# A new order for the first ten slots of a fused top-k attention and gated feed-forward kernel

## The chip, the cores and the metric

The kernel runs on one core of a Trainium2 chip. The core has five engines that work side by side, each through its own queue of instructions: TensorE (PE in the profile) multiplies matrices and loads weights for it (PEld), VectorE (DVE) and GpSimd (POOL) work on elements, ScalarE (ACT) evaluates functions and copies, SyncE (SP) starts transfers. The metric is the time of one execution on the device in microseconds (us), lower is better; a time given for a kernel is the median of its runs.

## The reference

There are 8 batches of 8 heads, 576 positions and 64 elements a head. For each query row the 576 scores are cut to the 32 largest, a softmax runs over those, and the values are summed with it. The heads of one position then stand side by side as a row of 512, and a feed-forward layer follows: 512 to 2048, a gate h * sigmoid(1.702 h), 2048 to 512.

```python
scores = scale * np.matmul(q, k.transpose(0, 1, 3, 2))          # (8, 8, 576, 576)
kth = np.partition(scores, -top_k, axis=-1)[..., -top_k:-top_k + 1]   # top_k = 32
scores = np.where(scores >= kth, scores, -1000000000.0)
attn = np.exp(scores - np.max(scores, axis=-1, keepdims=True))
attn = attn / (np.sum(attn, axis=-1, keepdims=True) + 1e-09)
x = np.matmul(attn, v)  # then (B, H, S, D) -> (B*S, H*D) = (4608, 512)
h = x @ w_in                                                    # (512, 2048)
g = h * (1.0 / (1.0 + np.exp(-1.702 * h)))
out = g @ w_out                                                 # (2048, 512)
```

## The kernel before

The work is cut into 144 slots, 18 for each batch. A slot is one tile of 128 query rows of a pair of heads (or the tails of two pairs). Five things are done with each slot's rows, in different slots of the program:

- **scores(n)**: 8 matmuls on TensorE and two copies out of PSUM on ScalarE.
- **topk(n)**: 14 operations on VectorE, eight MAX8 (each finds the 8 largest of 576) and six MATCH_REPLACE8 (each takes those out).
- **exponentials(n)** in slot n+1: two Prelu and two Exp on ScalarE, after the small bounds on GpSimd; then divide(n), which takes the reciprocal on VectorE in the middle of slot n+1's topk.
- **turn(n)** in slot n+1: the probabilities are transposed on TensorE and copied by ScalarE. In early slots the transposing matrix is the identity scaled by the reciprocals (`by`, made by GpSimd); in later ones it is the plain identity, and the probabilities are scaled before by ScalarE and GpSimd.
- **values(n)** in slot n+1: 10 matmul pairs on TensorE, one copy (xT) on ScalarE.

When the tiles of a row block are done, **hidden** computes a quarter of the feed-forward's first product per slot (16 matmuls), **tanh** and **gate** the gate in the slot after, and **project** a quarter of the second product (4 matmuls of 128x512) later. `to_project` is the queue in between. **prepare** transposes a pair of heads of q or k as it is loaded.

Both weight matrices, 32 pieces of 128x512, are loaded in the first slots and converted there into a form that TensorE takes: `size` (ScalarE), `shift` (VectorE), `sign` and `low` (ScalarE), and `finish` (two operations on GpSimd). A piece is loaded in the slot before its conversion, and finished in the slot after it. `by_slot` says how many pieces each slot converts.

Every engine works its queue in the order in which this program calls it, so the order of calls inside `slot(n)` is what the change is about. Blank lines are left out below, and cuts are marked.

```python
    SETTLED = 11
    # ... cut ...
    raws = pool("raws", 8)
    loads = pool("loads", 2)
    vals = pool("vals", 6)
    qkt = pool("qkt", 6)
    scp = pool("scp", 3)
    prp = pool("prp", 2)
    lefts = pool("lefts", 1)
    small = pool("small", 4)
    ptp = pool("ptp", 2)
    dgp = pool("dgp", 1)
    xtp = pool("xtp", 2)
    xtt = pool("xtt", 1)
    gtp = pool("gtp", 3)
    thp = pool("thp", 2)
    osp = pool("osp", 1)
    ps_s = pool("ps_s", 2, space=PSUM)
    ps_t = pool("ps_t", 2, space=PSUM)
    ps_h = pool("ps_h", 1, space=PSUM)
    ps_p = pool("ps_p", 1, space=PSUM)
    # ... cut ...
    pieces = [(c, g) for g in range(2) for c in range(CC)]
    for g in range(NG):
        pieces += [(c, g + 2) for c in range(CC) if g + 2 < NG] + [(None, f) for f in range(g * G, g * G + G)]
    # ... cut ...
    def round_piece(n):
        c, g = pieces[n]
        dst = wout[:, g, :] if c is None else win[:, c, g * PIECE : (g + 1) * PIECE]
        words = raw.pop(n)[:].rearrange("p (n w) -> p n w", w=2)
        low, high = words[:, :, 0], words[:, :, 1].bitcast(F32)
        bits, whole = dst.bitcast(U32), dst.bitcast(I32)
        def finish():
            nc.gpsimd.tensor_tensor(out=whole, in0=whole, in1=low.bitcast(I32), op=ALU.add)
            nc.gpsimd.tensor_tensor(out=dst, in0=dst, in1=high, op=ALU.mult)
        return {
            "size": lambda: nc.scalar.activation(dst, high, AF.Abs, scale=REBASE),
            "shift": lambda: nc.vector.tensor_scalar(bits, bits, 3, None, op0=ALU.logical_shift_left),
            "sign": lambda: nc.scalar.activation(high, high, AF.Sign),
            "low": lambda: nc.scalar.mul(out=low.bitcast(I32), in_=low, mul=2.0**-29),
            "finish": finish,
        }
    # ... cut ...
    def prepare(name, b, hp):
        src = loaded.pop((name, b, hp))
        before = 0 if name == "q" else TAIL
        dst = qkt.tile([P, S + before], F32, name=f"{name}_t")
        full = ps_t.tile([P, 512], F32, name="tp")
        for t in range(NF):
            nc.tensor.transpose(full[:, t * P : (t + 1) * P], src[:, t, :, :], ident[:])
        scale = SCALE if name == "q" else 1.0
        nc.scalar.mul(out=dst[:, before : before + FULL], in_=full[:], mul=scale)
        (qT if name == "q" else kT)[b, hp] = dst
        if name == "k":
            ends = ps_t.tile([P, 512], F32, name="tp")
            nc.tensor.transpose(ends[:, 0:P], loaded.pop(("ends", b, hp))[:], ident[:])
            nc.scalar.mul(out=qT[b, hp][:, FULL:S], in_=ends[:, 0:TAIL], mul=SCALE)
            for to in (0, before + FULL):
                nc.scalar.copy(out=dst[:, to : to + TAIL], in_=ends[:, TAIL:P])
    # ... cut ...
        sc = st[n]["sc"] = scp.tile([P, 2, S], F32, name="sc")
        for i in range(2):
            nc.scalar.copy(out=sc[:, i, :].rearrange("p (c k) -> p c k", c=2), in_=ps[i][:, :, 0:HALF])
    # ... cut ...
    def bounds(n):
        top = st[n]["top"]
        cut = st[n]["cut"] = small.tile([P, 2], F32, name="cut")
        low = st[n]["low"] = small.tile([P, 2], F32, name="low")
        nc.gpsimd.tensor_scalar(cut[:], top[:, :, TOPK - 1], -1.0, None, op0=ALU.mult)
        nc.gpsimd.tensor_tensor(out=low[:], in0=top[:, :, TOPK - 1], in1=top[:, :, 0], op=ALU.subtract)
    def exponentials(n):
        sc, cut, low = st[n]["sc"], st[n]["cut"], st[n]["low"]
        pr = st[n]["pr"] = prp.tile([P, 2 * S], F32, name="pr")
        den = st[n]["den"] = small.tile([P, 2], F32, name="den")
        for i in range(2):
            nc.scalar.activation(sc[:, i, :], sc[:, i, :], AF.Prelu, bias=cut[:, i : i + 1], alpha=HUGE)
        for i in range(2):
            nc.scalar.activation(
                pr[:, i * S : (i + 1) * S], sc[:, i, :], AF.Exp, bias=low[:, i : i + 1],
                accum_out=den[:, i : i + 1],
            )
    # ... cut ...
    def divide(n):
        den, pr = st[n]["den"], st[n]["pr"]
        some = small.tile([P, 2], F32, name="some")
        nc.vector.tensor_scalar_add(some[:], den[:], 1e-9)
        rden = small.tile([P, 2], F32, name="rden")
        nc.vector.reciprocal(rden[:], some[:])
        if n < SETTLED:
            by = st[n]["by"] = dgp.tile([P, 2, P], F32, name="by")
            for i in range(2):
                nc.gpsimd.tensor_scalar(by[:, i, :], ident[:], rden[:, i : i + 1], None, op0=ALU.mult)
        else:
            nc.scalar.activation(pr[:, 0:S], pr[:, 0:S], AF.Copy, scale=rden[:, 0:1])
            nc.gpsimd.tensor_scalar(pr[:, S : 2 * S], pr[:, S : 2 * S], rden[:, 1:2], None, op0=ALU.mult)
    # ... cut ...
    def tanh(aside):
        if to_gate:
            ph, g, rows = to_gate.pop()
            th = thp.tile([P, G, P], F32, name="th")
            nc.scalar.activation(th[:], ph[:], AF.Tanh, scale=0.851 / RAISE)
            if aside:
                h = raws.tile([P, G, P], F32, name="h", tag="raw")
                nc.scalar.copy(out=h[:], in_=ph[:])
                ph = h
            gated.append((th, ph, g, rows))
    def gate(aside):
        if not gated:
            return
        th, h, g, rows = gated.pop()
        gT = gtp.tile([P, G, P], F32, name="gT")
        if aside:
            nc.gpsimd.tensor_scalar(th[:], th[:], 1.0, None, op0=ALU.add)
            nc.gpsimd.tensor_tensor(out=gT[:], in0=th[:], in1=h[:], op=ALU.mult)
        else:
            nc.vector.scalar_tensor_tensor(
                out=gT[:], in0=th[:], scalar=1.0, in1=h[:], op0=ALU.add, op1=ALU.mult
            )
        to_project.append((gT, g, rows))
    # ... cut ...
    def project(blocks):
        if blocks[0] == 0:
            proj["on"] = to_project.pop(0)
    # ... cut ...
            ob = osp.tile([P, C], F32, name="ob")
            nc.scalar.mul(out=ob[:], in_=po[:], mul=0.5 / RAISE**2)
            for on, row in rows:
                nc.sync.dma_start(out[row : row + on.stop - on.start, :], ob[on, :])
    # ... cut ...
    by_slot = dict(enumerate([3, 4, 3, 4, 3, 4, 3, 4, 4]))
    # ... cut ...
            at(max(hp - 2, -1), load, name, 0, hp)
            at(max(hp - 2, -1), prepare, name, 0, hp)
    for hp in range(NP):
        at(hp - 1, load_v, 0, hp)
    for n in by_slot:
        for x in by_slot[n]:
            at(n - 1, load_piece, x)
    # ... cut ...
    def slot(n):
        todo = later.pop(n, [])
        for fn, args in todo:
            if fn is not prepare:
                fn(*args)
        preparing = [args for fn, args in todo if fn is prepare]
        settled = n > SETTLED
        aside = settled and n < N
        before = 0 <= n - 1 < N
        if before:
            bounds(n - 1)
            exponentials(n - 1)
        some = [round_piece(x) for x in by_slot.get(n, [])]
        for piece in some:
            piece["size"]()
        shifts = [piece["shift"] for piece in some]
        tanh(aside)
        for i, op in enumerate(topk(n) if 0 <= n < N else [lambda: None] * 14):
            op()
            if i == 2 and unfinished:
                unfinished.pop(0)()
            if i == 5:
                if before:
                    divide(n - 1)
                while unfinished:
                    unfinished.pop(0)()
            if i == 11 and not aside:
                gate(aside)
            if i > 6 and shifts:
                shifts.pop(0)()
        if aside:
            gate(aside)
        for args in preparing:
            prepare(*args)
        going = len(to_project) > (1 if n < N else 0)
        if going and settled:
            project(range(G - 1))
        if before:
            turn_main(n - 1)
        if going and settled:
            project(range(G - 1, G))
        if before:
            turn_ends(n - 1)
        for piece in some:
            piece["sign"]()
        if before:
            values(n - 1)
        for m in (0, 1) if n < 0 else (n + 2,):
            if m < N:
                scores(m)
        hidden()
        if going and not settled:
            project(range(G))
        for piece in some:
            piece["low"]()
            unfinished.append(piece["finish"])
    with tc.manual_schedule():
        for n in range(-1, N + 1):
            slot(n)
        n = N + 1
        while ready or to_gate or gated or to_project:
            slot(n)
            n += 1
```

Of the kernel before, what the change touches and what calls it, by code (L numbers as in the profile page):

```python
# [28 lines left out]
def kernel(  # L29
# [34 lines left out]
    CC = C // P  # L64
    FC = DFF // P
    G = 4
    NG = FC // G
# [4 lines left out]
    MAIN = (0, FULL + 2 * TAIL)  # L72
    SCALE = 1.0 / float(D) ** 0.5

    SETTLED = 11
    assert D == 64 and 2 * TAIL == P and C == NP * P and C == PIECE and B % 2 == 0
    assert TOPK == 32 and NP == 4 and NF == 4 and NG == 4 and CC == 4

# [1 line left out]
    pool = lambda name, bufs, **kw: ctx.enter_context(tc.tile_pool(name=name, bufs=bufs, **kw))  # L80
# [9 lines left out]
    dgp = pool("dgp", 1)  # L90
    xtp = pool("xtp", 2)
    xtt = pool("xtt", 1)
    gtp = pool("gtp", 3)
    thp = pool("thp", 2)
    osp = pool("osp", 1)
    ps_s = pool("ps_s", 2, space=PSUM)
# [7 lines left out]
    wout = const.tile([P, FC, C], F32, name="wout")  # L104


    pieces = [(c, g) for g in range(2) for c in range(CC)]
    for g in range(NG):
        pieces += [(c, g + 2) for c in range(CC) if g + 2 < NG] + [(None, f) for f in range(g * G, g * G + G)]
    raw = {}  # L110

    def load_piece(n):
# [8 lines left out]
# [26 lines that stand above are left out]
# [37 lines left out]
# [18 lines that stand above are left out]
# [8 lines left out]
    N = len(slots)  # L210
# [51 lines left out]
# [14 lines that stand above are left out]
# [5 lines left out]
# [3 lines that stand above are left out]
# [6 lines left out]
    def turn(n, first, cols, blocks):  # L290
# [5 lines left out]
        for c in range(blocks):  # L296
            at = slice(cols + c * P, cols + (c + 1) * P)
            if n >= SETTLED:
                nc.tensor.transpose(tp[:, c * P : (c + 1) * P], pr[:, at], ident[:])  # L299
# [15 lines left out]
    def turn_ends(n):  # L315

        turn(n, 2 * NF, FULL, 1)
# [3 lines left out]
    def values(n):  # L321
        b, t, hps = slots[n]
        pt = st[n]["pt"]
        outs = []
        for p in range(2 if t == NF else 1):
            cols = slice(p * TAIL, (p + 1) * TAIL) if t == NF else slice(0, P)
            main, tail = vv[b, hps[p]]
            o = ps_t.tile([P, 512], F32, name="o", tag="tp")
            for c in range(NF + 1):
                for j in range(2):  # L330
                    nc.tensor.matmul(  # L331
                        o[j * D : (j + 1) * D, 0 : cols.stop - cols.start],
                        lhsT=main[:, c, j, :] if c < NF else tail[:, j, :],
                        rhs=pt[:, j * NF + c if c < NF else 2 * NF, cols],
                        start=(c == 0),
                        stop=(c == NF),
                    )
            outs.append((o, hps[p]))
        for o, hp in outs:
            if t < NF:  # L340
                if (b, t) not in xts:
                    xts[b, t] = xtp.tile([P, CC, P], F32, name="xT")
                nc.scalar.copy(out=xts[b, t][:, hp, :], in_=o[:, 0:P])
            else:
                if (b // 2, t) not in xts:
                    xts[b // 2, t] = xtt.tile([P, CC, P], F32, name="xT_t")
                at = b % 2 * TAIL
                nc.scalar.copy(out=xts[b // 2, t][:, hp, at : at + TAIL], in_=o[:, 0:TAIL])
        if hps[-1] == NP - 1:
            if t < NF:  # L350
                ready.append((xts.pop((b, t)), [(slice(0, P), b * S + t * P)]))
            elif b % 2:
                rows = [(slice(i * TAIL, (i + 1) * TAIL), (b - 1 + i) * S + FULL) for i in range(2)]
                ready.append((xts.pop((b // 2, t)), rows))
        st[n].clear()
# [4 lines left out]
    to_gate, gated, to_project = [], [], []  # L360
# [77 lines left out]
    READY = (((-9, -8), (-7, -6), (-5, -4), (-3, -2)), ((-7, -6), (-5, -4), (-3, -3), (-2, -2)))  # L438
    FETCH = (((-13, -12), (-11, -10), (-7, -6), (-5, -4)), ((-11, -10), (-9, -8), (-6, -5), (-4, -3)))
    VALUES = ((-8, -7, -1, 0), (-8, -7, 0, 0))  # L440
    by_slot = dict(enumerate([3, 4, 3, 4, 3, 4, 3, 4, 4]))
    for n in by_slot:
        first = sum(map(len, list(by_slot.values())[:n]))
        by_slot[n] = list(range(first, first + by_slot[n]))
# [16 lines left out]
    unfinished = []  # L461
# [4 lines that stand above are left out]
            if fn is not prepare:  # L466
                fn(*args)
        preparing = [args for fn, args in todo if fn is prepare]
        settled = n > SETTLED
        aside = settled and n < N  # L470
        before = 0 <= n - 1 < N
        if before:
            bounds(n - 1)
            exponentials(n - 1)
        some = [round_piece(x) for x in by_slot.get(n, [])]
        for piece in some:
            piece["size"]()
# [14 lines that stand above are left out]
                shifts.pop(0)()  # L492
        if aside:
            gate(aside)
        for args in preparing:
            prepare(*args)
        going = len(to_project) > (1 if n < N else 0)
        if going and settled:
            project(range(G - 1))
        if before:  # L500
            turn_main(n - 1)
        if going and settled:
            project(range(G - 1, G))
        if before:
            turn_ends(n - 1)
        for piece in some:
            piece["sign"]()
        if before:
            values(n - 1)
        for m in (0, 1) if n < 0 else (n + 2,):  # L510
            if m < N:
                scores(m)
        hidden()
        if going and not settled:
            project(range(G))
        for piece in some:
            piece["low"]()
            unfinished.append(piece["finish"])

    with tc.manual_schedule():  # L520
        for n in range(-1, N + 1):
            slot(n)
        n = N + 1
# [33 lines left out]
```

## Time and profile before

| what | value |
|---|---|
| time, median of 3 runs | 1678.19 us (1676.68 to 1678.51) |
| span of the profiled run | 1674.9 us |
| VectorE busy in the profile | 1472.0 us |
| ScalarE busy | 1153.3 us |
| GpSimd busy | 746.3 us |
| one MAX8 or MATCH_REPLACE8 | 747 and 742 ns, next one starts some 70 ns before its end |
| matmuls of hidden, of project | 491.0 us in 4096 and 540.0 us in 1152 records |

In a line of the groups the profile names the line of the kernel, the engine, the operation, what it writes and what it reads, how often it ran, its busy time and the mean of one. A float32 product appears as two records, so 16 matmuls of `hidden` are 32 records. In a timeline the brackets hold the idle time before an instruction and who ended it. In a chain of waits each line is a start, a duration and what set the end in that stretch. TensorE's granted clock is given in tenths of full speed, or as a share of it.

### The profile page before, as it was taken

To read this page: it belongs to the slowest core of one execution; us is meant where nothing else is said; L and a number is where in the kernel's file an instruction comes from. 1 tells how busy PE (TensorE), PEld (TensorE's weight loads), DVE (VectorE), ACT (ScalarE), POOL (GpSimd) and SP (SyncE) were. 2 spreads that over 40 slices of the span, in tenths; PEclk is the share of its full clock that TensorE was granted. 3 is DMA by queue.
4 is the path that set the end of the run, shared out by engine and by line. 5 is a ranking of instruction groups with operands and counts; after the bars stand their busy time and mean duration, and the time that the engine had idled before them with its cause. 6 is when DMAs were issued, how large, how long until landed. Compare 5 with 4: busy or idle time off the path is not lost.

```text
span 1674.9 us, 32016 instructions
## 1 busy us (share of the span) xinstructions
PE 1599.7 (96%) x11945; PEld 1175.7 (70%) x11945; DVE 1472.0 (88%) x3212; ACT 1153.3 (69%) x2446; POOL 746.3 (45%) x783
## 2 busy tenths in 40 slices
PE   5577999999999999999999999999999999999999
PEld 3465767777777766777777776777777776777776
DVE  6898789998999997999899998999899998899990
ACT  6786566677766667667777776777776677666661
POOL 2776234444444443444444444444444443444440
PEclk7699999999999999999999999999999999999999
DMA  8342000111001110111001110011100110000000
GB/s 223 113 139 55 23 21 22 28 35 29 22 7 29 35 29 22 29 29 36 15 14 29 29 29 14 16 28 36 29 21 8 28 43 22 22 8 7 7 8 13
DMA packets 125723, 56.59 MB, mean 34 GB/s; under 512 B 116864, under 2 KB 116864, under 8 KB 125568
## 3 DMA queue, kind: packets, MB, share of 16 engines
q1 hardware_dynamic: 125568, 54.55, 12.3%
q8 instruction: 94, 1.54, 0.4%
q14 instruction: 61, 0.50, 0.1%
HBM read 45.09 MB, written 9.44 MB: 33 GB/s over the span
## 4 chain that ended last, share of the span: by engine, by line
PE 89%; ACT 6%; DVE 3%; issue 1%; SPq 1%; DMA 0%; POOL 0%; POOLq 0%
PE ph L372 29%; PE po L420 29%; PE o L331 10%; PE s_ps L224 10%; PE tp L299 8%; PE tp L301 2%; ACT pr L270 2%; PE tp L192 1%; ACT sc L231 1%; DVE top L240 1%; DVE left L243 1%; ACT sc L268 1%; ACT raw L144 1%; DVE wout L142 0%; ACT pr L287 0%
## 5 line engine op out<-in xcount | busy, mean ns | idle before, releaser
L240 DVE MAX8 top<-left 128x8 f32<-128x576 f32 x864 | 610.2, 747 | 0.0
L420 PE MATMUL po<-wout,gT 128*128 128x512 f32 x1152 | 540.0, 593 | 0.0
L288 POOL TENSOR_SCALAR pr<-pr,rden 128x576 f32<-128x576 f32 x133 | 229.5, 1725 | 683.3 <-ACT th L389 627.3
L372 PEld LDWEIGHTS ph<-xT,win 128*128 128x128 f32 x4096 | 467.2, 192 | 55.7 <-issue 47.4
L372 PE MATMUL ph<-xT,win 128*128 128x128 f32 x4096 | 491.0, 278 | 5.7 <-DVE gT L405 5.7
L243 DVE MATCH_REPLACE8 left<-top,left 128x576 f32<-128x576 f32 x576 | 423.3, 742 | 0.0
L309 ACT COPY pt<-tp 128x512 f32<-128x512 f32 (+1 forms) x432 | 193.5, 481 | 207.1 <-PE tp L299 183.0
L420 PEld LDWEIGHTS po<-wout,gT 128*128 128x128 f32 x1152 | 198.0, 191 | 143.5 <-issue 143.5
L231 ACT COPY sc<-s_ps 128x576 f32<-128x576 f32 x288 | 169.9, 642 | 130.1 <-PE s_ps L224 130.0
L270 ACT ACTIVATE pr<-sc,low 128x576 f32<-128x576 f32 x288 | 219.6, 768 | 0.0
L299 PEld LDWEIGHTS tp<-ident,pr 128*128 128x128 f32 x1197 | 142.9, 140 | 102.8 <-issue 41.5
L240 DVE MAX8 top<-sc 128x8 f32<-128x576 f32 x288 | 202.0, 743 | 13.8 <-ACT sc L231 13.8
L243 DVE MATCH_REPLACE8 left<-top,sc 128x576 f32<-128x576 f32 x288 | 211.6, 742 | 0.0
L268 ACT ACTIVATE sc<-sc,cut 128x576 f32<-128x576 f32 x288 | 208.7, 779 | 2.0 <-POOL cut L259 2.0
L402 POOL TENSOR_SCALAR th<-th 128x512 f32<-128x512 f32 x132 | 197.6, 1497 | 0.0
L224 PE MATMUL s_ps<-k_t,q_t 64*128 64x288 f32 (+1 forms) x1280 | 180.9, 430 | 1.2 <-ACT sc L231 0.7
L331 PEld LDWEIGHTS o<-pt,v_l 128*64 128x64 f32 x2560 | 127.9, 138 | 70.4 <-ACT pt L309 70.4
L299 PE MATMUL tp<-ident,pr 128*128 128x128 f32 x1197 | 174.6, 273 | 0.2 <-POOL pr L288 0.2
L403 POOL TENSOR_TENSOR gT<-th,h 128x512 f32<-128x512 f32 x132 | 168.9, 1280 | 11.0
L331 PE MATMUL o<-pt,v_l 128*64 128x128 f32 (+1 forms) x2560 | 161.8, 269 | 2.3 <-ACT pt L309 2.2
L279 DVE TENSOR_SCALAR some<-den 128x2 f32<-128x2 f32 x144 | 24.3, 169 | 147.4 <-ACT pr L270 147.3
L224 PEld LDWEIGHTS s_ps<-k_t,q_t 64*128 64x128 f32 (+1 forms) x1280 | 98.1, 177 | 41.0 <-issue 21.7
(50 smaller groups left out, 1171.3 us busy)
## 6 DMA issues: line engine op xcount, KB each, us to landing
q_l<-in_q_dram SPq DMA_DIRECT2D x64, 128.0 KB, 2.6
k_l<-in_k_dram SPq DMA_DIRECT2D x64, 128.0 KB, 2.6
v_l<-in_v_dram SPq DMA_DIRECT2D x64, 128.0 KB, 2.6
raw<-in_moe_w_in_dram SPq DMA_DIRECT2D x16, 512.0 KB, 4.7
raw<-in_moe_w_out_dram SPq DMA_DIRECT2D x16, 512.0 KB, 3.7
out_dram<-ob SPq DMA_DIRECT2D x32, 256.0 KB, 2.1
ends<-in_q_dram SPq DMA_DIRECT2D x32, 32.0 KB, 2.4
ends<-in_k_dram SPq DMA_DIRECT2D x32, 32.0 KB, 2.5
```

The lines of the kernel that those rows point to most:

```text
L224: nc.tensor.matmul(ps[i][rows, c, 0:HALF], lhsT=qT[b, hps[p]][on, cols], rhs=kT[b, hps[p]][on, FIRST[i] + c * HALF : FIRST[i] + (c + 1) * ...
L240: nc.vector.max(top[:, i, 8 * r : 8 * r + 8], (left if r else sc)[:, i, :])
L243: nc.vector.match_replace(left[:, i, :], top[:, i, 8 * r : 8 * r + 8], (left if r else sc)[:, i, :], LOWEST)
L268: nc.scalar.activation(sc[:, i, :], sc[:, i, :], AF.Prelu, bias=cut[:, i : i + 1], alpha=HUGE)
L270: nc.scalar.activation(pr[:, i * S : (i + 1) * S], sc[:, i, :], AF.Exp, bias=low[:, i : i + 1], accum_out=den[:, i : i + 1],)
L288: nc.gpsimd.tensor_scalar(pr[:, S : 2 * S], pr[:, S : 2 * S], rden[:, 1:2], None, op0=ALU.mult)
L299: nc.tensor.transpose(tp[:, c * P : (c + 1) * P], pr[:, at], ident[:])
L309: nc.scalar.copy(out=to, in_=tp[:, 0 : blocks * P])
L331: nc.tensor.matmul(o[j * D : (j + 1) * D, 0 : cols.stop - cols.start], lhsT=main[:, c, j, :] if c < NF else tail[:, j, :], rhs=pt[:, j * N ...
L372: nc.tensor.matmul(ph[:, i, :], lhsT=win[:, c, f * P : (f + 1) * P], rhs=xT[:, c, :], start=(c == 0), stop=(c == CC - 1),)
L402: nc.gpsimd.tensor_scalar(th[:], th[:], 1.0, None, op0=ALU.add)
L420: nc.tensor.matmul(po[:], lhsT=gT[:, i, :], rhs=wout[:, f, :], start=(f == 0), stop=(f == FC - 1))
```

## The change

The change reorders slots -1 to 9. It has four parts.

- **Scores first.** In slots -1 to 6 the preparation of a pair and the scores of slot n+2 come right after the exponentials, ahead of everything else. Before, they came after the values. In slot -1 each pair's scores follow its preparation directly.
- **Weight steps in ScalarE's waits.** `low` moves from the end of the slot to places ahead of `turn_main` (two pieces) and after `turn_ends` (the rest), where ScalarE would wait for TensorE. `sign` comes after the values' copy. The pieces are loaded in another order (three quarters of the first matrix, then a quarter of the second, and so on), and the slots take 2, 3, 4, 4, 4, 4, 3, 4, 4 pieces in place of 3, 4, 3, 4, 3, 4, 3, 4, 4.
- **Projections from slot 7 on, first in TensorE's slot.** Before, they began in slot 6 and stood last in TensorE's slot up to slot 11. Now they stand where the later slots have them, around `turn_main`. The queue `to_project` keeps two entries waiting and not one, so gT has four buffers and not three.
- **An earlier end of the early form.** Slots 9 and 10 of the probabilities are scaled ahead of a plain transpose, as all later ones; `SETTLED` goes from 11 to 9. The gate moves to GpSimd from slot 10 on, and not from slot 12 on.

The whole diff:

```diff
--- before.py
+++ after.py
@@ -72,7 +72,9 @@
     MAIN = (0, FULL + 2 * TAIL)
     SCALE = 1.0 / float(D) ** 0.5
 
-    SETTLED = 11
+
+    PROJECTS = 6
+    SETTLED = 9
     assert D == 64 and 2 * TAIL == P and C == NP * P and C == PIECE and B % 2 == 0
     assert TOPK == 32 and NP == 4 and NF == 4 and NG == 4 and CC == 4
 
@@ -90,7 +92,7 @@
     dgp = pool("dgp", 1)
     xtp = pool("xtp", 2)
     xtt = pool("xtt", 1)
-    gtp = pool("gtp", 3)
+    gtp = pool("gtp", 4)
     thp = pool("thp", 2)
     osp = pool("osp", 1)
     ps_s = pool("ps_s", 2, space=PSUM)
@@ -104,9 +106,8 @@
     wout = const.tile([P, FC, C], F32, name="wout")
 
 
-    pieces = [(c, g) for g in range(2) for c in range(CC)]
-    for g in range(NG):
-        pieces += [(c, g + 2) for c in range(CC) if g + 2 < NG] + [(None, f) for f in range(g * G, g * G + G)]
+    pieces = [(c, g) for g in range(NG - 1) for c in range(CC)] + [(None, f) for f in range(G)]
+    pieces += [(c, NG - 1) for c in range(CC)] + [(None, f) for f in range(G, FC)]
     raw = {}
 
     def load_piece(n):
@@ -438,7 +439,7 @@
     READY = (((-9, -8), (-7, -6), (-5, -4), (-3, -2)), ((-7, -6), (-5, -4), (-3, -3), (-2, -2)))
     FETCH = (((-13, -12), (-11, -10), (-7, -6), (-5, -4)), ((-11, -10), (-9, -8), (-6, -5), (-4, -3)))
     VALUES = ((-8, -7, -1, 0), (-8, -7, 0, 0))
-    by_slot = dict(enumerate([3, 4, 3, 4, 3, 4, 3, 4, 4]))
+    by_slot = dict(enumerate([2, 3, 4, 4, 4, 4, 3, 4, 4]))
     for n in by_slot:
         first = sum(map(len, list(by_slot.values())[:n]))
         by_slot[n] = list(range(first, first + by_slot[n]))
@@ -466,12 +467,22 @@
             if fn is not prepare:
                 fn(*args)
         preparing = [args for fn, args in todo if fn is prepare]
-        settled = n > SETTLED
-        aside = settled and n < N
+        settled = n > PROJECTS
+        aside = SETTLED < n < N
         before = 0 <= n - 1 < N
         if before:
             bounds(n - 1)
             exponentials(n - 1)
+        if n < 0:
+            for m in range(2):
+                for args in preparing:
+                    if args[2] == m:
+                        prepare(*args)
+                scores(m)
+        elif not settled:
+            for args in preparing:
+                prepare(*args)
+            scores(n + 2)
         some = [round_piece(x) for x in by_slot.get(n, [])]
         for piece in some:
             piece["size"]()
@@ -492,30 +503,30 @@
                 shifts.pop(0)()
         if aside:
             gate(aside)
-        for args in preparing:
-            prepare(*args)
-        going = len(to_project) > (1 if n < N else 0)
-        if going and settled:
+        if settled:
+            for args in preparing:
+                prepare(*args)
+        for piece in some[:2]:
+            piece["low"]()
+        going = settled and len(to_project) > (2 if n < N else 0)
+        if going:
             project(range(G - 1))
         if before:
             turn_main(n - 1)
-        if going and settled:
+        if going:
             project(range(G - 1, G))
         if before:
             turn_ends(n - 1)
+        for piece in some[2:]:
+            piece["low"]()
+        if before:
+            values(n - 1)
         for piece in some:
             piece["sign"]()
-        if before:
-            values(n - 1)
-        for m in (0, 1) if n < 0 else (n + 2,):
-            if m < N:
-                scores(m)
+            unfinished.append(piece["finish"])
+        if settled and n + 2 < N:
+            scores(n + 2)
         hidden()
-        if going and not settled:
-            project(range(G))
-        for piece in some:
-            piece["low"]()
-            unfinished.append(piece["finish"])
 
     with tc.manual_schedule():
         for n in range(-1, N + 1):
```

## The prediction

> **What bounds the kernel now.** I read the page's busy shares and its 40 slices first, then windows of equal length, then the chain of waits inside the first 170 us, then the timeline around the first slots.
>
> From the page of the kernel before (busy time by engine; then the span in 40 slices of 42 us, busy tenths, and the granted TensorE clock):
>
> ```profile
> PE 1599.7 (96%) x11945; PEld 1175.7 (70%) x11945; DVE 1472.0 (88%) x3212; ACT 1153.3 (69%) x2446; POOL 746.3 (45%) x783
> ...
> PE   5577999999999999999999999999999999999999
> PEclk7699999999999999999999999999999999999999
> ```
>
> TensorE is the bound from the fifth slice on. Only the first four slices, some 170 us, have holes, and the change lies in them. The windows (length, busy time of each engine, clock, DMA share, GB/s) say the same:
>
> ```profile
> 40.00:60.00 20.00, 8.03 (x52) 6.37 (x48) 16.80 (x33) 16.07 (x32) 14.76 (x16) 0.68 0.36 120
> 100.00:120.00 20.00, 16.72 (x118) 13.54 (x117) 19.83 (x42) 17.39 (x35) 16.48 (x19) 0.91 0.40 134
> 300.00:600.00 300.00, 300.00 (x2194) 220.56 (x2191) 277.47 (x613) 212.67 (x451) 134.29 (x140) 1.00 0.11 27
> ```
>
> At 40 to 60 us no engine is full: a ring of waits. At 100 to 120 VectorE is full (19.83 of 20). From 300 TensorE is. So the end is the moment at which TensorE becomes saturated, plus the TensorE work still undone then. The ring is in the chain (start, duration, what), slots 2 to 3:
>
> ```profile
> 52.27 2.13 PE o L331 x20
> 54.41 1.22 PE s_ps L224 x8
> 55.63 1.16 ACT sc L231 x2
> 56.79 1.67 ACT raw L144 x3
> 58.46 0.70 ACT sc L268 x2
> 59.16 0.52 issue
> 59.68 1.62 ACT pr L270 x4
> 61.33 0.18 DVE some L279
> ...
> 61.87 0.62 POOL by L285
> 62.48 0.04 issue
> 62.53 3.80 PE tp L301 x16
> ```
>
> Scores and their copies (1.22 + 1.16) stand in the ring between the values of one slot and the exponentials of the next. I call the start of a slot's first MAX8 of its scores T(n). In the timeline T(0) to T(11) are 13.84, 24.51, 39.66, 55.45, 70.89, 84.90, 100.19, 113.70, 128.13, 142.38, 152.88 and 170.53. The 17.65 us of slot 10 come from this piece of the chain:
>
> ```profile
> 157.16 3.45 PE po L420 x8
> 160.61 0.02 issue
> 160.64 0.60 ACT ob L425
> 161.23 0.71 ACT sc L268 x2
> 161.94 0.52 issue
> 162.46 1.62 ACT pr L270 x4
> ```
>
> The output copy ob stands ahead of the exponentials in ScalarE's order and waits for a projection that is last in TensorE's slot. TensorE is then empty from 160.6 to 165.3.
>
> **What the Trainium skill says.** "TensorE: Matmul & The Clock Gate", Part 1: after an idle window of about 3.4 us the array runs at half rate, until it has worked for about as long again. The trace agrees: the 16 matmuls of L301 take 3.80 us in the chain after 7 us of idling, 1.80 us at 148.45 without it. The same page, in its part on the array's sub-arrays, calls ScalarE and VectorE strictly first in, first out. The trace agrees in the ob wait just shown, and my estimate of slot 0 rests on it. "SBUF — State Buffer", section "Who interferes with whom": VectorE in its two-port mode and GpSimd lock each other out for a whole instruction. The shift of a weight piece (L142) agrees: 0.41 us while GpSimd is empty at 19 us, median 0.84, up to 1.54 beside GpSimd's rounding. So a weight piece costs VectorE some 0.75 us a shift, and a reorder can't remove it.
>
> **The change part by part, slots 0 to 9.** Nothing is computed less, except that slots 9 and 10 get transposes in place of products with a scaled identity.
>
> (a) Start. Scores 0 no longer wait for the second pair. ScalarE's ends copies of pair 0 end near 8.3; scores take 2.3 (row at 10.85) and the first copy 0.67, so T(0) is about 11.3: 2.5 earlier.
>
> (b) Slot 0. The two size steps now follow pair 2's preparation and scores 2 in ScalarE's queue, and VectorE's first shift stands after its eighth operation. The k load of pair 2 landed at 20.23. There is now one 512 KB piece less ahead of it; at 263 to 313 GB/s (windows of 4 us from 12 to 20 us) that is 1.8 us, so 18.4. Transposes 1.1 and copies 1.05 make 20.6, scores 2.3, copies 1.2, first size 0.65: 24.75. VectorE reaches its shift at 11.3 + 5.6 = 16.9, so it stands for about 7.8 us. From the first shift to the end of slot 0 were 5.11 us with three shifts, 4.8 with two: T(1) = 29.5, 5.0 later than before.
>
> (c) Slot 1. Exponentials end at 33.0; copies of pair 3 take 1.7; scores cold 2.3, their copies 1.2, first size 0.65: 38.9. The shift was reachable at 35.6. T(2) = 38.9 + 5.1 = 44.0, 4.3 later.
>
> (d) Slots 2 to 5, four pieces each. ScalarE's load is exponentials 2.95, scores 1.18, sizes 2.35, lows 2.4 (half of it beside TensorE), turn copies and their waits 1.8, x copy 0.25, signs 2.35, and the values of TensorE, 1.3 to 2, that half of the lows hides: 14.2 us in sum. VectorE needs, from the timeline, 4.1 to its reciprocal and 9.56 after it: 13.7, and 0.6 more with a gate. So the ring goes from 14.7 to 15.3 down to 14.2 or 14.8, ScalarE sets it by half a microsecond, and T(3) to T(6) are about 59.6, 73.8, 88.0, 102.8.
>
> (e) Slots 6 to 8 stay with VectorE (13.5 to 14.4 before): T(7) 116.8, T(8) 131.0, T(9) 145.3. That is 2.9 later than before. What the ring gives back (60.5 to 58.8 us from T(2) to T(6)) does not pay for slots 0 and 1.
>
> (f) Slots 9 and 10. Projection first in the slot takes TensorE's 3.44 us out of the place before the next exponentials. From T(9): gate and hidden(9) begin at +11.4 (before +10.9), end at +15.1, projection to +17.7; GpSimd, still rounding, gives the bounds at +13.6 as before, so exponentials end at +17.2, the scaling at +19.4; transposes 0.87, last projection block 0.86, ob and the pt copies about 1.0, values 1.24, scores 1.17: hidden(10) at +24.1, that is 169.4 against 172.3. From there slots are full: hidden(11) 10.95 later, hidden(12) another 11.06 later, at 191.4 against 199.66. Gain 8.3.
>
> (g) Owed. At that point one projection more is undone, since the backlog is two and not one: 3.44 us. In the tail, where TensorE is full to the last two projections, it is paid in full. Net: 8.3 - 3.4 = 4.9 us. The fourth gT buffer only holds the longer backlog.
>
> So 1678.2 - 5 = 1673, rounded.
>
> **The rivals.** First, slot 0 doesn't stall: the pair-2 loads land some 5 us sooner, or VectorE's stand is short. Then T(1) is near 22, slots follow at VectorE's pace (12.8, then four of 13.7 to 14.3), T(9) near 138, and the gain is 12 to 16 us: 1662 to 1666. For it: two pieces instead of three are ahead in the queue, and the change's aim is that ScalarE waits there. Against it: the transfers already ran at 263 to 313 GB/s from 12 to 20 us, and two queues that keep their order leave no way around.
>
> Second, GpSimd becomes the bound. Four pieces at 2.65 to 2.9 us each, the scaled identity 1.2 and bounds 0.4 make 12.7 to 13.4 of a 14 us slot, now in slots 3 to 6 without a light slot between. Bounds come late, and each slot stretches by up to 1 us; T(9) near 149, and the change costs nothing or 1 us: 1677 to 1679.
>
> Third, the raw buffers: eight, with four per slot, so a load waits for the rounding of two slots ago, and a size step could wait for it. I think the landing comes 3 to 5 us before its use. If not, it adds to the second rival.
>
> **Range and chances.** The stage can hardly give more than its holes: up to 160 us TensorE is idle some 40 us, but VectorE's own work in slots 0 to 8 is about 121 us (10.8, 12.8, three of 13.7, 14.3, 13.5, two of 14.3) and stays. A 2% change is 33 us, twice the best rival. I put 0.25 on the first rival, 0.2 on the second or third, the rest around 1673: range 1664 to 1680; faster by 2% 0.02, within 2% 0.97, slower 0.01.
>
> **What would show it.** In the profile after: VectorE's L142 in slot 0 waiting some 7 us for ScalarE's L142 size step (if it waits under 3, step (b) is wrong and the first rival holds); T(1) near 29.5, T(2) near 44; slots 2 to 5 at 14.2 to 14.8 with VectorE waiting under 1 us for the exponentials; T(9) near 145; no hole at ob, hidden(10) near 169, hidden(12) near 191; three projections at the end in place of two. If steady slots change their 10.6 to 11.1 us, the whole frame is wrong.

## The result, and the profile after

| | before | changed kernel |
|---|---|---|
| time, median | 1677.43 us (4 runs) | 1669.72 us (4 runs, 1668.71 to 1670.05) |
| ratio to before | 1 | 0.9953, 95% interval 0.9936 to 0.997 |
| the same, measured again later | 1677.18 us (9 runs) | 1667.04 us (5 runs), ratio 0.9942, 0.993 to 0.9955 |
| span of the first profile | 1674.9 us | 1667.9 us |

The change saves 7.7 us in the first measurement and 10.1 in the second. The page of the changed kernel (busy time, then 40 slices of 42 us):

```profile
PE 1599.2 (96%) x11923; PEld 1174.2 (70%) x11923; DVE 1468.8 (88%) x3210; ACT 1155.7 (69%) x2450; POOL 753.0 (45%) x785
...
PE   5579999999999999999999999999999999999999
PEclk7789999999999999999999999999999999999999
```

TensorE's busy time is what it was (1599.7 before); its fourth slice went from 7 to 9. The windows (length, busy time of TensorE, weight loads, VectorE, ScalarE and GpSimd, clock, DMA share, GB/s):

```profile
40.00:60.00 20.00, 10.10 (x82) 7.64 (x81) 19.84 (x41) 18.83 (x38) 12.17 (x14) 0.83 0.30 98
100.00:120.00 20.00, 15.64 (x119) 12.58 (x119) 18.31 (x40) 16.38 (x33) 15.80 (x17) 0.97 0.48 156
```

From 40 to 60 us VectorE is now full (19.84, it was 16.80): the ring of waits is gone there. The chain of waits shows it in slots 2 and 3 (start, duration, what):

```profile
55.88 2.64 DVE top L241 x4
58.52 1.45 DVE left L244 x2
59.97 1.33 DVE top L241 x2
...
61.40 0.15 DVE rden L282
61.55 1.46 DVE left L244 x2
63.01 1.46 DVE win L143
```

Nothing but VectorE stands in it. But VectorE pays earlier. Its timeline, where a bracket is the idle time ahead of an instruction and who ended it:

```profile
24.85 0.43 DVE L143 TENSOR_SCALAR win<-win 128x512 uint32<-128x512 uint32 x1 [8.55 <-ACT win L142]
...
29.63 1.40 DVE L241 MAX8 top<-sc 128x8 f32<-128x576 f32 x2
...
38.13 0.43 DVE L143 TENSOR_SCALAR win<-win 128x512 uint32<-128x512 uint32 x1 [2.61 <-ACT win L142]
...
43.25 1.40 DVE L241 MAX8 top<-sc 128x8 f32<-128x576 f32 x2
```

It stands for the first size step, 8.55 us in slot 0 and 2.61 us in slot 1. The sums of its waits up to slot 9 are close: before 13.8 us until the first scores and 8.0 for exponentials; after 10.7, then 11.2 for size steps in slots 0 and 1 and 1.6 in slot 6. So T(9), the start of slot 9, is 142.01 in place of 142.38. The early half of the change has gained 0.4 us by then, which is less than two profiles of the changed kernel differ by (142.01 and 140.83). The rest comes in slots 9 and 10, where the chain is now this:

```profile
154.37 1.30 POOL wout L139
155.66 0.20 POOL cut L260
155.89 0.82 ACT sc L269 x2
...
159.70 0.79 ACT pr L288
160.53 0.66 PE tp L300 x4
```

No output copy stands between the bounds and the exponentials. The exponentials start at 155.89, 3.39 us after T(10); before, it was 8.25 us. What is left of this wait is GpSimd's, in both kernels: it gives slot 9's bounds 3.14 us after T(10), when its last rounding is done. Of TensorE's timeline before, this is the line behind the hole:

```profile
165.30 3.78 PE L301 MATMUL tp<-by,pr 128*128 128x128 f32 x16 [4.71 <-POOL by L285]
```

The hole of 4.71 us is gone, as the projection now runs up to 160.5, where the transposes begin. The starts of hidden(n) on TensorE:

| slot n | before | after | earlier by |
|---|---|---|---|
| 8 | 141.18 | 140.81 | 0.4 |
| 9 | 153.32 | 154.06 | -0.7 |
| 10 | 172.30 | 165.17 | 7.1 |
| 11 | 185.00 | 176.21 | 8.8 |
| 12 | 199.59 | 187.36 | 12.2 |
| 51 | 628.96 | 616.73 | 12.2 |
| 52 | 642.39 | 632.13 | 10.3 |
| 144 | 1639.71 | 1629.24 | 10.5 |

Of the 12.2 us, 3.44 are owed, because one projection more is undone. They are paid at the end, where TensorE's timeline has 24 records in one row (16 before, 7.03 us):

```profile
1653.93 10.46 PE L421 MATMUL po<-wout,gT 128*128 128x512 f32 x24
```

Another 1.8 us are lost from slot 51 on, with a slow projection in slot 51 that the repetition takes up. 12.2 - 3.4 - 1.8 is the 7.0 us by which the span shrank.

### The profile page after: what moved, and what is told of

Read it like the earlier page. It is cut to its first block, busy times and chain, and to the rows that moved or that the text cites. A ratio compares the mean times of both kernels' runs of the same rounds, so it can differ in the third digit from the quotient of the medians.

```text
span 1667.9 us, 31998 instructions
## 1 busy us (share of the span) xinstructions
PE 1599.2 (96%) x11923; PEld 1174.2 (70%) x11923; DVE 1468.8 (88%) x3210; ACT 1155.7 (69%) x2450; POOL 753.0 (45%) x785
## 4 chain that ended last, share of the span: by engine, by line
PE 87%; DVE 5%; ACT 5%; SPq 1%; issue 1%; POOL 1%; DMA 0%; POOLq 0%; ACTq 0%
PE ph L373 29%; PE po L421 29%; PE o L332 10%; PE s_ps L225 10%; PE tp L300 8%; DVE top L241 2%; DVE left L244 2%; ACT pr L271 1%; PE tp L193 1%; ACT sc L232 1%; DVE wout L143 1%; ACT sc L269 1%; ACT pr L288 0%; SPq L160 0%; DVE win L143 0%
## 5 line engine op out<-in xcount | busy, mean ns | idle before, releaser
L289 POOL TENSOR_SCALAR pr<-pr,rden 128x576 f32<-128x576 f32 x135 | 232.9, 1725 | 688.8 <-ACT th L390 640.7
L241 DVE MAX8 top<-sc 128x8 f32<-128x576 f32 x288 | 201.9, 742 | 10.7 <-ACT sc L232 10.7
L404 POOL TENSOR_TENSOR gT<-th,h 128x512 f32<-128x512 f32 x134 | 171.5, 1280 | 11.2
L280 DVE TENSOR_SCALAR some<-den 128x2 f32<-128x2 f32 x144 | 24.1, 168 | 130.6 <-ACT pr L271 130.4
```

What stands on the lines that cost most here:

```text
L241: nc.vector.max(top[:, i, 8 * r : 8 * r + 8], (left if r else sc)[:, i, :])
```

## The experiments

Times are medians. The kernel before was 1676.95 us in the first group, 1677.76 in the second and 1677.18 in the third.

### The two halves

**The late half alone**, built on the kernel before:

```diff
-    SETTLED = 11
+    PROJECTS = 6
+    SETTLED = 9
-    gtp = pool("gtp", 3)
+    gtp = pool("gtp", 4)
-        settled = n > SETTLED
-        aside = settled and n < N
+        settled = n > PROJECTS
+        aside = SETTLED < n < N
-        going = len(to_project) > (1 if n < N else 0)
+        going = settled and len(to_project) > (2 if n < N else 0)
-        if going and not settled:
-            project(range(G))
```

> The kernel before, with the late half of the change alone: projections from slot 7 on, first in TensorE's slot, two waiting, SETTLED 9; slots -1 to 6 and the weight pieces as before. Theory A (the whole gain comes from slots 9 to 11, where the output copy no longer holds up the exponentials and transposes are cheaper; the early half arrives at slot 9 no sooner): T(9) near 142, hidden(10) 7 us earlier than before, time 1668 to 1671, as the whole change. Rival B (both halves carry a share, the early order by letting TensorE work ahead): 1672 to 1675.

Measured: 1668.1 us, ratio 0.9943 (0.9931 to 0.9956). T(9) is 141.90 and hidden(12) starts at 187.25; in the changed kernel they were 142.01 and 187.36. Theory A holds: this half gives the whole gain.

**The early half alone**, the changed kernel with these edits:

```diff
-    SETTLED = 9
+    SETTLED = 11
-        going = settled and len(to_project) > (2 if n < N else 0)
+        going = len(to_project) > (1 if n < N else 0)
-        if going:                       # both places
+        if going and n > SETTLED:
         hidden()
+        if going and n <= SETTLED:
+            project(range(G))
```

> The changed kernel, with the late half undone: projections from slot 6 on, last in TensorE's slot up to slot 11, one waiting, SETTLED 11; scores first and the weight steps as changed. Theory A: the stand of VectorE in slot 0 (8.6 us) and slot 1 (2.6 us) eats what slots 2 to 5 give back, the hole behind the output copy in slot 10 remains, time 1676 to 1679, as before. Rival B: 1672 to 1675.

Measured: 1676.5 us, ratio 0.9994 (0.9986 to 1.0002). T(9) is 142.07, and the output copy is back in the chain at 160.32. B falls.

**The late half without the earlier transposes**: as the first, but `SETTLED` stays 11.

> The late half without the earlier transposes: projections first from slot 7, two waiting, but SETTLED stays 11, so slots 9 and 10 of the probabilities keep the product with the scaled identity and the gate stays on VectorE up to slot 11. Theory A1 (the place of the projection closes the hole of 4.7 us and the cold matmuls behind it; the transposes are worth their own 1.1 us a slot, two slots): 1671 to 1673. Rival A2 (the transposes carry most, since GpSimd's scaled identity comes late behind the rounding): 1674 to 1677.

Measured: 1669.1 us (0.9935 to 0.996 of before), 2 us better than A1 said. From T(9) to hidden(12) it takes 46.88 us, where the full late half takes 45.35. These 1.5 us are what the transposes are worth beside the moved projection; in the medians it is 1.0 us. The products of slot 10 start 18.31 us after T(9), where it was 22.92 before, and with no hole of 4.71 us ahead of them the 16 take 1.95 us and not 3.78.

**SETTLED 9 alone**, one line of the kernel before.

> The kernel before with SETTLED 9 alone: slots 9 and 10 of the probabilities by transposes, gate on GpSimd from slot 10, projection first only from slot 10 on, one waiting. The projection of slot 9 is still last, so its output copy still stands ahead of the exponentials of slot 9. Theory A1: the hole remains, 2 us less TensorE work: 1675 to 1677. Rival A2: 1671 to 1673.

Measured: 1670.36 us (0.9944 to 0.9969), which is just under A2's range, and only in part for A2's reason. TensorE's timeline of this kernel around the hole:

```profile
157.09 3.60 PE L420 MATMUL po<-wout,gT 128*128 128x512 f32 x8
161.37 2.84 PE L420 MATMUL po<-wout,gT 128*128 128x512 f32 x6 [0.69 <-ACT ob L425]
165.84 1.33 PE L299 MATMUL tp<-ident,pr 128*128 128x128 f32 x8 [1.62 <-ACT pr L287]
```

The output copy still holds the exponentials up: the transposes start at 165.84, no earlier than the products of before at 165.30. But slot 10 is now the one in which the projection moves from last to first, so two projections come together, and most of the second one runs in the hole. In the kernel before the two came together in slot 12, where TensorE had no hole. hidden(10) is 1.8 us earlier, hidden(11) 3.5, hidden(12) 6.9. Nothing is owed here, as the queue holds one entry.

The starts in the timelines divide the 6.9 us (parts rounded). Six of the projection's records in the hole are 2.6. The way from the start of the transposes to hidden(10) is 3.78 us without the projection's other two records (0.86). Before, the way from the products was 7.00, so this is 3.2. From hidden(10) to hidden(11) it is 11.04 in place of 12.70: 1.7. The later start costs 0.5. So the transposes carry the larger share here, though beside the moved projection they are worth 1.5: alone, they also replace the 16 products that ran slow behind the hole (3.78 us, against 1.95 in slot 9).

So each of the two late edits alone gives most of the gain, at the same place: one closes the hole, the other fills part of it and shortens what comes behind it. Together they give 1.0 and 2.3 us more than each alone. No run separates the place of the projection from the second entry left waiting and the fourth gT buffer.

### What the early half could give

Six kernels try to shorten VectorE's stands and waits. The first four were not measured beside the changed kernel, which was 1669.72 us in the result and 1667.04 in the last group. The size steps ahead of preparation and scores:

```diff
+        some = [round_piece(x) for x in by_slot.get(n, [])]
+        for piece in some:
+            piece["size"]()
         if n < 0:
             # ... cut: preparation and scores ...
-        some = [round_piece(x) for x in by_slot.get(n, [])]
-        for piece in some:
-            piece["size"]()
```

> The changed kernel with the size steps ahead of the preparation and the scores in slots 0 to 6. Theory C (the early half earns nothing because VectorE stands for the size steps, and moving them only passes the wait on): the stands of 8.6, 2.6 and 1.6 us in slots 0, 1 and 6 go, but ScalarE then reaches the exponentials of slots 0 and 1 late, since it still waits for the pair loads; VectorE waits 3 to 4 us for them in each of slots 1 and 2, T(3) near 55.8 in place of 57.1, T(9) near 139 in place of 142, time 3 us under the changed kernel's. Rival D (the stands are the whole cost): T(9) near 130, time 10 to 12 us under.

Measured: 1664.52 us, ratio 0.992 (0.9905 to 0.9935). The stands shrink to 0.55 us in slot 0 and to nothing later. In their place VectorE waits 3.85 and 2.59 us for exponentials; T(3) is 54.25 and T(9) 137.73. ScalarE's timeline shows the first of them:

```profile
23.33 1.18 ACT L232 COPY sc<-s_ps 128x576 f32<-128x576 f32 x2 [2.04 <-PE s_ps L225]
24.39 1.23 ACT L145 ACTIVATE raw<-raw 128x512 int32<-128x512 uint32 x2
25.51 1.21 ACT L144 ACTIVATE raw<-raw 128x512 f32<-128x512 f32 x2
26.60 1.44 ACT L269 ACTIVATE sc<-sc,cut 128x576 f32<-128x576 f32 x2
```

Slot 1 began at 21.57, but ScalarE still waited for pair 2's scores, and lows and signs of slot 0 follow ahead of the exponentials. Theory C holds, D falls.

The same in slot 6 alone (`if n == 6` around the earlier place):

> The changed kernel with the size steps ahead of the scores in slot 6 alone. Theory: the wait of 1.62 us in slot 6 goes, T(7) to T(9) come 1.6 us earlier, and since GpSimd's rounding gives the bounds of slot 9 that much earlier too, the time falls by 1.6 us one to one. Rival: the rounding on GpSimd is the bound by then, T(9) moves and hidden(10) doesn't; time unchanged.

Measured: 1667.88 us, 1.8 us under the changed kernel's first median. It looked like the theory, until the changed kernel itself was measured again: 1667.04 us, and its profile has no wait in slot 6. That wait came from hidden(5), which took 5.66 us in the first profile, at a granted clock of 0.50 from 97 to 100 us, and 3.84 in the second; the scores of slot 8 stand behind it (the first profile, then the second):

```profile
97.43 5.66 PE L373 MATMUL ph<-xT,win 128*128 128x128 f32 x32 [0.79 <-DVE gT L406]
```

```profile
97.63 3.84 PE L373 MATMUL ph<-xT,win 128*128 128x128 f32 x32 [1.92 <-DVE gT L406]
```

So the edit isn't shown to do anything.

No piece in slot 0:

```diff
-    by_slot = dict(enumerate([2, 3, 4, 4, 4, 4, 3, 4, 4]))
+    by_slot = dict(enumerate([0, 4, 4, 4, 4, 4, 4, 4, 4]))
```

> The changed kernel with no weight piece in slot 0 and four in each of slots 1 to 8. Theory C: slot 0 takes 10.0 us without its stand, T(1) near 20.7; in slot 1 VectorE then waits 2.4 us for the exponentials and 4 us for the size steps behind pair 3 and its scores; T(3) near 54, T(9) near 139, time 3 us under the changed kernel's. Rival D: T(9) near 133, 8 us under.

Measured: 1665.88 us, ratio 0.9927 (0.9911 to 0.9944). T(1) is 20.35, but VectorE then stands 7.59 us for the size step of slot 1; T(3) is 53.91, T(9) 139.65, with a wait of 1.46 us in slot 6 behind a hidden(5) of 5.50 us. C's picture holds and D falls; how much time it saves is open, 1.2 us against the changed kernel's second median and 3.8 against its first.

No piece in slot 0, the size steps ahead of preparation and scores, and the scores of slot 3 a slot later (the diff shows this last part):

```diff
-            scores(n + 2)
+            for m in {1: (), 2: (3, 4)}.get(n, (n + 2,)):
+                scores(m)
```

> As the one without pieces in slot 0, and the size steps ahead of preparation and scores in all slots, and the scores of slot 3 moved from slot 1 to slot 2. Theory C: no stand in slot 0, none for size steps later, and slot 1 loses its cold scores and their copies; VectorE waits 2.4 us for the exponentials in slot 1 and under 1 us in slots 2 and 3. T(3) near 51, T(9) near 135, time 6 to 8 us under the changed kernel's. Rival E (GpSimd, with four pieces a slot and never three, is the bound): T(9) near 139, 3 us under or less.

Measured: 1663.33 us, ratio 0.9914 (0.9899 to 0.9928). No stand for size steps is left, but VectorE waits 6.22 us for exponentials in slot 2 and 2.34 in slot 3. T(3) is 51.43 as expected and T(9) 138.10, not 135. Four pieces a slot without a pause don't bind GpSimd: slots 4 to 8 take 13.6 to 14.2 us, as in the changed kernel. Neither C nor E had the 6.22 us.

Pairs 2 and 3 loaded a slot earlier:

```diff
-            at(max(hp - 2, -1), load, name, 0, hp)
+            at(max(hp - 3, -1), load, name, 0, hp)
 # ... cut: pair 2 is loaded into buffers of raws ...
```

> The version with no piece in slot 0 and the scores of slot 3 in slot 2, and the loads of pairs 2 and 3 one slot earlier, pair 2 in free weight buffers. In the run without this, VectorE waits 6.2 us in slot 2 and 2.3 us in slot 3 for the exponentials, since the k load of pair 3 lands at 28.0 and its transposes stand ahead of turn(0) in TensorE's queue. Theory F (the pair loads are what is left of the start): the 6.2 us fall to about 2, T(9) near 134 to 136, time 2 to 4 us lower, 1659 to 1661. Rival G (the weight pieces now land later, and the wait goes over to them; ScalarE's own work of the first nine slots is the bound): T(9) near 138, 1662 to 1664.

Measured: 1664.37 us, ratio 0.9924 (0.9911 to 0.9936). G: the pair lands sooner and the weights land later. ScalarE now waits 1.08, 0.55, 0.90 and 0.69 us for the four pieces of slot 1, the last size step ends at 29.5, and turn(0) starts at 30.60, where it was 29.98 without this. VectorE's wait in slot 2 is 5.69 us, T(9) 137.41.

The preparation of pair 3 in slot 2 instead:

```diff
-            at(max(hp - 2, -1), prepare, name, 0, hp)
+            at((-1, -1, 0, 2)[hp], prepare, name, 0, hp)
```

> The version with no piece in slot 0 and the scores of slot 3 in slot 2, and the preparation of pair 3 moved to slot 2 as well, its load unchanged. Theory F: turn(0) starts 4 us earlier, the wait in slot 2 falls to about 2, but slot 2 takes over the four copies of pair 3 (1.7 us) and the wait in slot 3 grows to 4 or 5: T(9) near 136 to 137, 1661 to 1662. Rival G: what is taken from one slot comes back whole in the next, T(9) near 138, 1663.

Measured: 1662.49 us, ratio 0.9913 (0.9899 to 0.9926), the lowest median of all, though the ratio is not told apart from the 0.9914 of the version with that preparation in slot 1; the changed kernel was 1667.04 beside it. The wait in slot 2 falls to 1.22 us, that of slot 3 grows to 5.42; T(3) is 46.58 and T(9) 136.30. F's T(9) and waits hold nearly, its time lies just over what F said, and G is in part right on the mechanism: of the 5.0 us gained in slot 2, 3.1 come back in slot 3.

### The repetition

> The changed kernel itself once more, beside the one with the late half alone. Both had hidden(12) at the same moment (187.36 and 187.25), and yet the times were 1669.7 and 1668.1, with a slow stretch of projections near 623 us in the profile of the changed kernel alone, after an idle time of 1.95 us. If that stretch belongs to this kernel's timing, it is there again and the time is again 1.5 us over the other; if it comes and goes by chance, the two medians meet within 0.7 us.

> The kernel with the late half alone, once more, for the comparison with the changed kernel: 1668.1 as before if the difference is steady.

Measured: 1667.04 us for the changed kernel, 1667.87 for the late half alone. They are 0.8 us apart, a little over the 0.7 said, and in the other direction. So the 1.6 us of the first measurement belong to neither. TensorE's timeline in slot 51, first the first profile of the changed kernel, then the second:

```profile
623.38 0.39 PE L199 MATMUL tp<-ident,ends 128*128 128x128 f32 x1 [1.95 <-ACT q_t L195]
623.56 4.42 PE L421 MATMUL po<-wout,gT 128*128 128x512 f32 x6
```

```profile
622.19 0.33 PE L199 MATMUL tp<-ident,ends 128*128 128x128 f32 x1 [1.94 <-ACT q_t L195]
622.35 2.74 PE L421 MATMUL po<-wout,gT 128*128 128x512 f32 x6
```

The same idle time was followed once by a projection of 4.42 us, with a granted clock of 0.83 from 620 to 630, and once by one of 2.74. Whether an idle time of 1.9 us costs 1.7 us more is decided by something that the order of instructions doesn't set. In the profiled runs it accounts for the whole distance, as the next table shows; that it does so in the medians is likely, but not shown.

The second profile also shows what bounds slot 9. TensorE got to its projection there 2.5 us sooner, and then stood for the scaled probabilities:

```profile
159.35 1.33 PE L300 MATMUL tp<-ident,pr 128*128 128x128 f32 x8 [1.36 <-ACT pr L288]
```

In both profiles the transposes start 18.52 us after T(9). So with the output copy out of the way it is the chain from GpSimd's bounds through the exponentials that sets hidden(10), and not TensorE.

### What T(9) decides

| kernel | T(9) | hidden(12) | hidden(12) - T(9) | time, median | profiled run - T(9) |
|---|---|---|---|---|---|
| before | 142.38 | 199.59 | 57.2 | 1677.4 | 1534.3 |
| early half alone | 142.07 | 199.40 | 57.3 | 1676.5 | 1534.2 |
| SETTLED 9 alone | 142.47 | 192.66 | 50.2 | 1670.4 | 1527.7 |
| late half without the earlier transposes | 140.99 | 187.87 | 46.9 | 1669.1 | 1527.4 |
| changed kernel, first | 142.01 | 187.36 | 45.4 | 1669.7 | 1527.7 |
| changed kernel, second | 140.83 | 186.18 | 45.4 | 1667.0 | 1526.0 |
| late half alone, first | 141.90 | 187.25 | 45.4 | 1668.1 | 1526.1 |
| no piece in slot 0 | 139.65 | 185.01 | 45.4 | 1665.9 | 1525.7 |
| the same, sizes first, scores of slot 3 in slot 2 | 138.10 | 183.47 | 45.4 | 1663.3 | 1525.7 |
| the same, pair 3 prepared in slot 2 | 136.30 | 181.65 | 45.4 | 1662.5 | 1525.7 |

The last column is the time of the one run that was profiled, less its T(9). The first three have one projection more behind them at hidden(12), which is 3.44 us of the difference. In the ten profiles with the full late half the way from T(9) to hidden(12) is 45.33 to 45.37 us. In nine of them the profiled run takes 1525.7 to 1526.1 us from T(9) on, and in the tenth, the first of the changed kernel, 1527.7: the 1.7 us of the slow projection. So T(9) passes to the time one to one.

## Why the prediction was right

The range and the direction held (1673, range 1664 to 1680, measured 1669.7 and 1667.0), and so did the late half's mechanism. The centre missed by 3 to 6 us: 1667.0 is nearer to the first rival's 1662 to 1666 than to 1673, so the time alone would not have told the two apart. VectorE's stand of 8.55 us does. By its steps:

- **(a) to (c) right.** T(0) was 10.66 (said 11.3), the stand in slot 0 was 8.55 us (7.8), T(1) 29.63 (29.5), the stand in slot 1 2.61 us (3.3), T(2) 43.25 (44.0). The first rival, a short stand, is out.
- **(d) mis-sized.** Slots 2 to 5 took 13.88, 13.63, 13.64 and 14.23 us; I had said 15.6, then 14.2, 14.2 and 14.8. I took ScalarE's sum as the pace, and it is not. The terms as listed give 13.4 to 14.1 and not 14.2, and the first 15.6 has no term behind it. In slot 4 ScalarE worked from 71.55 to 84.59, 13.0 us: exponentials, copies, sizes, lows and signs were as said, but behind the lows the copy of the values waited only 0.09 us, where I had left up to 0.8. Then ScalarE stood 0.61 us for the bounds, which follow VectorE's last MAX8. So VectorE set the pace, with its 13.7. T(6) was 98.63, not 102.8. Slots 2 to 5 of the kernel before had taken 14.0 to 15.8 us, not 14.7 to 15.3.
- **(e) off by one wait.** Slot 6 took 14.87 us and not 14.0, since scores first stand behind hidden(5), which waits for the gate and ran slow. This one comes and goes. T(9) was 142.0, not 145.3. So the ring does pay for slots 0 and 1, but with nothing over, and the late half alone gives what the whole gives.
- **(f) right in mechanism.** No hole at the output copy; the bounds at T(9) + 13.6, as said; hidden(10) at T(9) + 23.2 (said 24.1, though its terms add up to 24.5), and the next ones 11.04 and 11.15 us later (10.95 and 11.06). The gain at hidden(12) was 12.2 us (from 199.59, not 199.66) in place of 8.3, and 3.3 of the 3.9 us between are the error in T(9).
- **(g) right.** 3.44 us, three projections at the end. A gain without this debt is possible: the kernel with SETTLED 9 alone owes nothing and gains 6.6 us.
- **The second and third rival fall.** Slots 4 to 8 with four pieces each took 13.6 to 14.2 us in the kernel with the scores of slot 3 in slot 2, so GpSimd keeps up (the second rival's own terms add up to 12.2 to 13.2 us, not 12.7 to 13.4). GpSimd is late once, with the bounds of slot 9, and by the same 3.1 us in every kernel. In the changed kernel no size step waited for a load.
- **The room was larger than said.** TensorE is idle 52.7 us of the first 160 in the kernel before (busy 107.33), not some 40.

What I did not see: that the two late edits are largely substitutes, each worth 6.6 to 7.9 us alone and 8.9 together.

## What to carry to other kernels

In a pipeline whose last bound is one engine, ask what a reorder does to the moment at which that engine becomes full, and measure that moment; what slots 2 to 5 gained here was paid back in slots 0 and 1, and the time came from one hole behind an output copy that stood ahead of the wrong instruction in a queue. Work that must be done sometime is free in a hole, so look for holes before removing them. Before a step is moved to where its engine waits, ask whether another engine waits for that step in order: VectorE stood 8.6 us for a step of 0.65 us.

## What was not expected of the hardware

After an idle time of 1.95 us TensorE ran slow once (a projection took 4.42 us in place of 2.74), and after 1.94 us in the same place of the same program it didn't. In the two profiles of the late half alone hidden(8) took 5.47 us after 2.23 us of idling and 3.84 after 2.22. "TensorE: Matmul & The Clock Gate", Part 1, in the Trainium skill says that the window is free-running, which would make it a matter of phase; the runs show the two outcomes, not their cause. The idle window that this page gives, about 3.4 us, is longer than all these idle times, so here the measurement decides: shorter ones were followed by a low rate, in some executions and not in others. Rates that differ in this way, at hidden(5), moved T(9) of one unchanged kernel from 142.01 to 140.83, and five profiles with slots -1 to 6 as before have T(9) from 140.99 to 142.47. So differences under 1.5 us between two profiles here mean nothing by themselves.
